# Six units' transposed keys: TensorE transposes and a copy in place of VectorE transposes and a trip through DRAM

## The chip, the cores and the metric

The kernel runs on one core of one Trainium2 chip. The metric is the device time of one execution in microseconds; before the change it is 614.58 us, the median of three runs (614.53 to 615.55). Engines are called by the names of the profile: PE is TensorE (PEld its weight loads), DVE is VectorE, ACT is ScalarE, POOL is GpSimd, SP the engine whose queue issues most of the DMAs.

## What is computed

A gated linear attention with a running state, and a SwiGLU block on its output, all in fp32. In the reference, cut to what matters:

```python
batch, n_heads, seq, head_dim = (4, 8, 768, 48)      # q, k, v, f_logit
n_tokens, d_model, d_ff = (3072, 384, 1536)
...
f = 1.0 / (1.0 + np.exp(-f_logit))
for t in range(S):
    state = f[:, :, t, :, None] * state + np.einsum('bhd,bhe->bhde', k[:, :, t], v[:, :, t])
    y[:, :, t] = np.einsum('bhd,bhde->bhe', q[:, :, t], state)
...
x = np.ascontiguousarray(attn_out.transpose(0, 2, 1, 3)).reshape(B * S, H * D)
g = x @ w_gate
silu = g * (1.0 / (1.0 + np.exp(-g)))
return (silu * (x @ w_val) @ w_out)
```

## The kernel before

**Units and chunks.** The sequence is cut into six chunks of 128 tokens (NCH = 6). A unit is one batch in one chunk, with all eight heads; units are numbered u = 4c + b, 24 in all. `attention(u)` computes one unit and is a Python generator: each `yield` ends a step, and the caller decides when the next step's instructions are put into the program. Eight heads are held as four pairs (HP = 4), two heads on 128 partitions.

**The steps of a unit** (from the third chunk on, c >= 2): the sigmoid of f (L555, ACT), a 32x32 block transpose of f on DVE (L561), the same of k (L568), the backward running product `tail` of the gates and its reciprocal (L572 to L577), the multiplication kT = k * tail (L582), the forward running product in the place of the gates (L596), the transpose of q (L599) and the multiplication into qT (L602). Then PE makes the scores of the pairs, sc = kT^T qT (L615, eight matmuls of 48 rows), DVE applies the causal mask (L628), PE adds the output y from the decayed state and the masked scores (L649, L653, or L674 for the last batch of a chunk), ACT copies y out (L657, L689), and PE adds the state's sum dS from `kt` and v (L694). `kt` is kT turned: tokens on the partitions, heads times 64 along the row. The last chunk needs no dS and no `kt`.

**Two ways to `kt`.** For most units PE transposes kT in four matmuls against the identity into a PSUM bank right after the scores (L616 to L619), and ACT copies the bank to SBUF (L626). Units 14 to 19 (`turned`, L584) do otherwise: DVE turns 32x32 blocks of kT into the room that qT will take (L589), four DMAs on SP's queue store that to DRAM (`turn`, L592), and after the scores one DMA reads it back in the other order as `kt` (L624). qT's own transpose (L599) has to wait until the four stores have read its room.

**The MLP of chunk c runs while the attention of chunk c+1 goes on.** The first chunk's MLP is plain. From the second on it uses sums of blocks: four triples of 15 products (`triple`, L954, names A, B, o, c for the banks that the products go to), each product two matmuls of 256 columns, then seven down products in fourteen halves (L1053, L1116). ACT copies the banks out as `c..` or `aside` tiles (L959; three `aside` rooms), DVE adds and subtracts them (L855, L858), ACT applies SiLU (L970) and DVE multiplies (L906).

**PSUM.** From the second chunk's MLP on there are two banks of kind A, one of kind B, two of kind o, and three in a pool of their own for y, dS and kt (`later`). Scores stand in banks borrowed from the kinds A and o (`score_bank`), as the table `SCORES` says.

**What sets the order.** A planner by due times: the pieces of the MLP carry an estimated duration (PRODUCT 0.86 us, DOWN 3.9 us), and each step of `attention` has a due time relative to the start of the MLP chunk beside which it runs. `chain(k, q, qmul, turn, head)` (L819) gives the times of a unit's DVE steps: k + STEPS, then `turn` (L589 and L592) and `head` (L596), both k + 3.5 where not given, then q (L599) and qmul (L602). `CHAINS` holds them by chunk and batch, `times` (L835) makes the list of a unit's steps. Whenever the planner's clock has passed a step's due time, `come_in` puts the step in. At the end `in_order` (L1283) pins each engine's instructions to the order in which they were put in, SP's queue among them. Otherwise the framework's scheduler may order what has no dependency.

The names that the change touches are `turn_pool` (L321), the steps L584 to L594 and L616 to L626, the state's sum's operand (L695), the numbers of steps in `attention_steps` (L715) and `run` (L1172), `STEPS`, `chain` and `CHAINS`, and the last call of `in_order`.

Of the kernel before, what the change touches and what calls it, by code (L numbers as in the profile page):

```python
# [9 lines left out]
FP32 = mybir.dt.float32  # L10
# [279 lines left out]
def short_path(ctx, tc, ident, least, judge, q, k, v, f_logit, moe_w_gate, moe_w_val, moe_w_out, out):  # L290
# [9 lines left out]
    nc = tc.nc  # L300
    B, H, S, D = q.shape
    C = 128
    NCH = S // C
    HP = H // 2
    W = 64
# [9 lines left out]
    SQUARES = 2  # L315
# [2 lines left out]
    const = ctx.enter_context(tc.tile_pool(name="const", bufs=1))  # L318
    att = ctx.enter_context(tc.tile_pool(name="att", bufs=1))
    ffn = ctx.enter_context(tc.tile_pool(name="ffn", bufs=2))  # L320
    turn_pool = ctx.enter_context(tc.tile_pool(name="turn", bufs=2, space=bass.MemoryType.DRAM))  # L321
    sums_pool = ctx.enter_context(tc.tile_pool(name="sums", bufs=1))

    early = ctx.enter_context(ExitStack())
# [25 lines left out]
    start = const.tile([128, HP * N1], FP32, tag="start", name="start")  # L350
# [42 lines left out]
    Q = 32  # L393
    NI = C // Q
# [9 lines left out]
    def v_of(u):  # L404
        return vs[u % (NV if units[u][1] < SQUARES else NV // 2)]
# [105 lines left out]
    def rows_of(par):  # L511
        return slice(W * par, W * par + D)
# [3 lines left out]
    def bank(name):  # L516
        return banks[-1].tile([128, 512], FP32, tag="a", name=name)
# [10 lines left out]
    def attention(u):  # L528
        b, c = units[u]
        fr, kr, qr = (raw[nm][u % NRAW] for nm in "fkq")  # L530
        v_ = v_of(u)
# [15 lines left out]
        def transposed(name, src):  # L547
            p = bank(name)
            for a in range(HP):
                nc.tensor.transpose(p[:, a * C:(a + 1) * C],  # L550
                                    src[:, 2 * a:2 * a + 2, :].rearrange("t r d -> t (r d)"), ident)
            return p.rearrange("p (a t) -> p a t", t=C)
# [3 lines left out]
        else:  # L556
            p = transposed("fTp", fr)
# [6 lines left out]
        kT = att.tile([128, HP, C], FP32, tag="kT", name="kT")  # L564
        qT = att.tile([128, HP, C], FP32, tag="qT", name="qT", bufs=2)
# [15 lines left out]
            qp = transposed("qTp", qr)  # L581
        nc.vector.tensor_tensor(kT, kp, pairs(tail, 2)[:, :, 0:C], ALU.mult)  # L582
        yield
        turned = (SQUARES + 1) * B + 1 < u < (NCH - 1) * B  # L584
        if turned:


            beside = qT.rearrange("p a t -> p (a t)").rearrange("p (i m) -> p i m", i=NI)
            nc.vector.transpose(beside.rearrange("p i (a e) -> p a i e", e=Q), kT.rearrange("p a (i e) -> p a i e", e=Q))  # L589
            turn = turn_pool.tile([Q, NI, HP, NI, Q], FP32, tag="turn", name="turn")  # L590
            for r in range(NI):
                nc.sync.dma_start(out=turn[:, :, :, r, :].rearrange("t i a e -> t (i a) e"),  # L592
                                  in_=beside[Q * r:Q * (r + 1)].rearrange("t i (a e) -> t (i a) e", e=Q))
        yield  # L594

        nc.vector.tensor_tensor_scan(gate[:, 0:n], gate[:, 0:n], start, 1.0, op0=ALU.mult, op1=ALU.add)  # L596
        yield
# [14 lines left out]
        for a in range(HP):  # L612
            for par in range(2):
                r = rows_of(par)
                nc.tensor.matmul(sc[par][:, a * C:(a + 1) * C], lhsT=kT[r, a, :], rhs=qT[r, a, :], start=True, stop=True)  # L615
        if c < NCH - 1 and not turned:  # L616
            p = bank("kt")
            for a in range(HP):
                nc.tensor.transpose(p[:, a * C:(a + 1) * C], kT[:, a, :], ident)  # L619
        yield  # L620
        if c < NCH - 1:
            kt = att.tile([128, HP * C], FP32, tag="kt", name="kt")
            if turned:
                nc.sync.dma_start(out=kt, in_=turn.rearrange("t i a r e -> i t (a r e)"))  # L624
            else:
                nc.scalar.copy(kt, p)  # L626
        for par in range(2):
            nc.vector.tensor_tensor(A[:, par], sc[par].rearrange("p (a t) -> p a t", t=C),  # L628
                                    causal.unsqueeze(1).broadcast_to((128, HP, C)), ALU.mult)
# [7 lines left out]
        if c and b < B - 1:  # L637
# [8 lines left out]
            for a in range(HP):  # L646
                for par in range(2):
                    r = rows_of(par)
                    nc.tensor.matmul(place(a, par), lhsT=decayed[r, a, :], rhs=qT[r, a, :],  # L649
                                     start=a < 2, stop=False, skip_group_check=True)  # L650
            for par in range(2):
                for a in range(HP):
                    nc.tensor.matmul(place(a, par), lhsT=v_[:, 2 * a + par, :], rhs=A[:, par, a, :],  # L653
                                     start=False, stop=a >= HP - 2, skip_group_check=True)
# [3 lines left out]
            for h in range(H):  # L658
                a, par = h // 2, h % 2
                f = h * D  # L660
                while f < (h + 1) * D:
                    n = min((h + 1) * D, (f // 128 + 1) * 128) - f
                    r = W * (a % 2) + f - h * D
                    nc.sync.dma_start(out=xT[c][f % 128:f % 128 + n, f // 128, b * C:(b + 1) * C],
                                      in_=yT[r:r + n, par, a // 2 * C:(a // 2 + 1) * C])
                    f += n
        else:
# [15 lines left out]
            for par in range(2):  # L683
                for n in range(DM // Q):
                    h = n // per * 2 + par
# [5 lines left out]
        if c < NCH - 1:  # L691
            p = bank("dS")
            for h in range(H):
                nc.tensor.matmul(p[W * (h % 2):W * (h % 2) + W, (h // 2) * D:(h // 2 + 1) * D],  # L694
                                 lhsT=kt[:, h * W:(h + 1) * W], rhs=v_[:, h, 0:D], start=True, stop=True)  # L695
            dS = p[:, 0:HP * D].rearrange("p (a d) -> p a d", d=D)
        if c >= SQUARES and u + 2 < len(units):
            load(u + 2, "v")
# [13 lines left out]
    def attention_steps(c):  # L712

        runs = [attention(c * B + b) for b in range(B)]
        parts = [3, 6, 3, 3]  # L715
        order = sorted((2 * b + s, b, n) for b in range(B) for s, n in enumerate(parts))
        return [lambda b=b, n=n: [next(runs[b]) for _ in range(n)] for _, b, n in order]

# [2 lines left out]
    def in_order(since, engines):  # L721

        start = len(traced)
        while traced[start - 1] is not since:
            start -= 1
        for engine in engines:
            keep_order([ins for ins in traced[start:] if ins.engine == engine])

    def keep_order(mine):
        for a, b in zip(mine, mine[1:]):  # L730
            tc.add_manual_dep(b, a.name, mybir.DependencyInfo(mybir.DependencyClass.NoSync,
                                                              mybir.DependencyReason.DATA), reason="order")
# [80 lines left out]

    STEPS = (-1.3, 0, 1.3, 2.8)
    TRIPLE = PRODUCT * 15

    def chain(k, q, qmul, turn=None, head=None):  # L819
        return (*[k + t for t in STEPS], turn or k + 3.5, head or k + 3.5, q, qmul)  # L820

    whole = NJ * TRIPLE + 7 * DOWN
    between = [n * TRIPLE - 0.05 for n in range(NJ)]
# [4 lines left out]
        *[((down[10] - whole, "A"), (between[1], "o"), (between[3], "o"), (down[3], "A"))] * (NCH - 4)))}  # L828
    CHAINS = {c: chains for c, chains in zip(range(2, NCH), (
        (chain(2.6, 4, 9), chain(14.5, 20, 23), chain(30, 37, 44), chain(57.4, 59, 61)),  # L830
        (chain(-12, -8.5, -5), chain(3.5, 6, 9), chain(16, 28, 33, 21.5, 23.5), chain(40.1, 53, 55, 44.5, 52)),
        *[(chain(-19.4, -11.2, -9.5), (-7.5, -6.3, 1.3, 2.2, 3.2, 5.5, 8, 10), chain(16, 28, 33, 21.5, 23.5), chain(40.1, 53, 55, 44.5, 52))] * (NCH - 4)))}
    LAST = 72.5

    def times(c):  # L835
# [327 lines left out]
    mark = traced[-1]  # L1163
    keep_warm(5)
    first = [attention(b) for b in range(B)]
    done = [0] * B

    def run(b, *steps):
        for s in steps:
            assert done[b] == s  # L1170
            done[b] += 1
            for _ in range((3, 1, 5, 3, 3)[s]):  # L1172
                next(first[b])

    def load_ahead(u):
# [5 lines left out]
        if u + NRAW == B:  # L1181
            load(u + NRAW, "fkq")

    run(0, 0, 1, 2)
    load_ahead(0)
    for b in range(1, B):
        if b == 1:
            run(1, 0)
            keep_warm(6)
        run(b, 1)  # L1190
        run(b - 1, 3)
        run(b, 2)
        load_ahead(b)
        if b + 1 < B:
            run(b + 1, 0)
        else:
            sizes.pop(0)()
        run(b - 1, 4)
# [6 lines left out]

    hidden, last = mlp_plain(0)
    steps = attention_steps(1)
    sigmoid_ahead(B)
    joins.pop(0)()
# [38 lines left out]
    mark = traced[-1]  # L1248
    waiting = []
    for c in range(2, NCH):  # L1250
        for b in range(B):
            run = attention(c * B + b)
            waiting += [((c - 2) * whole + t, lambda run=run: next(run)) for t in times(c)[b]]
# [26 lines left out]
            now += took  # L1280
    for g in lagging:
        g()
    in_order(mark, (mybir.EngineType.PE, mybir.EngineType.DVE, mybir.EngineType.Activation, mybir.EngineType.Pool, mybir.EngineType.SP))  # L1283


@with_exitstack
def kernel(
# [22 lines left out]
    def judge(bank):  # L1310
# [12 lines left out]
        yield  # L1323

    short_path(tc, ident, least, judge, *args)
    with tc.If(redo[0] > 0):
        general_path(tc, *args)
# [32 lines left out]
```

## Time and profile before

| | us |
|---|---|
| median of three runs | 614.58 |
| the profiled execution | 615.55 |
| its span on the core | 613.7 |
| L619, PE transposes of kT: 56, each record | 0.273 |
| L626, ACT copy of kt, 14 | 0.586 |
| L589, DVE transpose of kT, 6 | 0.704 |
| L596, DVE running product, 24, mean | 1.224 |
| L592, stores of `turn`, issue of each of 24 | 0.626 |
| L592, issue to landing, median | 2.6 |
| L624, load of `kt`, issue of each of 6 | 0.602 |

The profile is one execution, and its span lies within that execution's time. A row "x56" is the number of instructions, and for one instruction the record's duration is given. Records of matmuls overlap, so the distance from one group's start to the next one's is what a group takes on PE. In the timeline a line has start, duration, engine, source line, operation and tile; lines of one kind that follow each other are merged. An fp32 matmul shows as two records there (the eight score matmuls of a unit as "x16", a product's two as "x4"), a transpose as one ("x4" for a unit's four).

### The profile page before, as it was taken

To read this page: it belongs to the slowest core of one execution; us is meant where nothing else is said; L and a number is where in the kernel's file an instruction comes from. 1 tells how busy PE (TensorE), PEld (TensorE's weight loads), DVE (VectorE), ACT (ScalarE), POOL (GpSimd) and SP (SyncE) were. 2 spreads that over 40 slices of the span, in tenths; PEclk is the share of its full clock that TensorE was granted. 3 is DMA by queue.
4 is the path that set the end of the run, shared out by engine and by line. 5 is a ranking of instruction groups with operands and counts; after the bars stand their busy time and mean duration, and the time that the engine had idled before them with its cause. 6 is when DMAs were issued, how large, how long until landed. Compare 5 with 4: busy or idle time off the path is not lost.

```text
span 613.7 us, 10812 instructions
## 1 busy us (share of the span) xinstructions
PE 596.7 (97%) x4036; PEld 488.6 (80%) x4036; DVE 499.5 (81%) x882; ACT 285.1 (46%) x526; POOL 7.6 (1%) x51
## 2 busy tenths in 40 slices
PE   7799999999999999999999999999999999999996
PEld 4654545666888799888899988899988899988895
DVE  7799989878999996989997889996879991566731
ACT  2375646312776520576731376641276730366600
POOL 1000000000000000000000000000000000000000
PEclk9899999999999999999999999999999999999999
DMA  9999582005322144324235344145313100100001
GB/s 150 246 209 284 175 249 79 1 14 154 85 54 69 27 97 115 113 53 96 52 96 129 98 111 108 33 112 118 110 43 91 27 5 10 52 2 2 1 0 58
DMA packets 109143, 54.10 MB, mean 88 GB/s; under 512 B 68761, under 2 KB 102169, under 8 KB 109081
## 3 DMA queue, kind: packets, MB, share of 16 engines
q1 hardware_dynamic: 107064, 50.56, 34.6%
q10 hardware_dynamic: 2016, 2.75, 1.2%
q8 instruction: 34, 0.56, 0.4%
q14 instruction: 29, 0.23, 0.1%
HBM read 44.04 MB, written 6.29 MB: 82 GB/s over the span
## 4 chain that ended last, share of the span: by engine, by line
PE 85%; DVE 7%; DMA 3%; ACT 2%; issue 1%; SPq 1%; ACTq 0%; DVEq 0%
PE o L1053 19%; PE A L954 14%; PE B L954 11%; PE gate L752 5%; PE val L752 5%; PE o L775 5%; PE o L954 5%; PE c L954 4%; PE sc L615 4%; PE o L1116 3%; PE y L653 2%; PE y L674 2%; PE dS L694 1%; PE y L649 1%; DVE c L858 1%; DMA fraw<-in_f_logit_dram 1%
## 5 line engine op out<-in xcount | busy, mean ns | idle before, releaser
L954 PE MATMUL A<-xs,w_both 128*128 128x256 f32 x240 | 62.5, 383 | 1.2 <-ACT aside L959 1.2
L1053 PE MATMUL o<-w_out,h 128*128 128x192 f32 x360 | 62.0, 327 | 0.5 <-DVE h L906 0.5
L1053 PEld LDWEIGHTS o<-w_out,h 128*128 128x128 f32 x360 | 58.7, 190 | 1.7 <-DVE h L906 0.8
L959 ACT COPY c<-A 128x512 f32<-128x512 f32 x40 | 23.3, 583 | 66.8 <-PE A L954 66.8
L954 PEld LDWEIGHTS A<-xs,w_both 128*128 128x128 f32 x240 | 44.5, 190 | 9.1 <-ACT aside L959 2.8
L855 DVE TENSOR_TENSOR c<-c,aside 128x512 f32<-128x512 f32 x60 | 41.4, 691 | 9.8 <-ACT aside L959 8.4
L959 ACT COPY aside<-A 128x512 f32<-128x512 f32 x60 | 35.0, 583 | 28.9 <-PE A L954 28.9
L906 DVE TENSOR_TENSOR h<-h,c 128x256 f32<-128x256 f32 x100 | 41.1, 419 | 7.9 <-ACT h L970 7.7
L970 ACT ACTIVATE h<-c 128x256 f32<-128x256 f32 x100 | 39.2, 416 | 9.0 <-DVE c L855 5.8
L858 DVE TENSOR_TENSOR c<-c,aside 128x512 f32<-128x512 f32 x60 | 41.3, 688 | 2.0 <-ACT aside L959 1.7
L954 PE MATMUL B<-xs,w_both 128*128 128x256 f32 x160 | 41.2, 380 | 0.7 <-ACT aside L959 0.7
L1053 PE MATMUL o<-ws,h 128*128 128x192 f32 x240 | 41.5, 328 | 0.2 <-DVE A L628 0.2
L954 PE MATMUL c<-xT,w_both 128*128 128x256 f32 x160 | 41.2, 380 | 0.5 <-DVE c L858 0.5
L954 PE MATMUL A<-xs,extra 128*128 128x256 f32 x160 | 41.2, 380 | 0.0
L954 PE MATMUL B<-xT,extra 128*128 128x256 f32 x160 | 41.1, 379 | 0.0
L628 DVE TENSOR_TENSOR A<-sc,causal 128x512 f32<-128x512 f32 x48 | 30.8, 684 | 11.3 <-PE sc L615 11.3
L959 ACT COPY aside<-B 128x512 f32<-128x512 f32 x60 | 35.0, 584 | 10.2 <-PE B L954 7.2
L1053 PEld LDWEIGHTS o<-ws,h 128*128 128x128 f32 x240 | 39.1, 190 | 0.8 <-DVE A L628 0.4
L858 DVE TENSOR_TENSOR c<-o,c 128x512 f32<-128x512 f32 x40 | 27.7, 693 | 10.2 <-ACT h L970 5.8
L954 PEld LDWEIGHTS B<-xs,w_both 128*128 128x128 f32 x160 | 30.2, 190 | 5.2 <-ACT aside L959 1.1
L954 PEld LDWEIGHTS c<-xT,w_both 128*128 128x128 f32 x160 | 30.2, 190 | 5.1 <-DVE c L858 0.9
L954 PEld LDWEIGHTS A<-xs,extra 128*128 128x128 f32 x160 | 30.3, 190 | 4.4 <-ACT c L959 0.3
(137 smaller groups left out, 1139.8 us busy)
## 6 DMA issues: line engine op xcount, KB each, us to landing
fsquares<-in_f_logit_dram SPq DMA_DIRECT2D x64, 96.0 KB, 2.6
ksquares<-in_k_dram SPq DMA_DIRECT2D x64, 96.0 KB, 2.4
qsquares<-in_q_dram SPq DMA_DIRECT2D x64, 96.0 KB, 2.3
v<-in_v_dram SPq DMA_DIRECT2D x24, 192.0 KB, 3.5
w<-in_moe_w_gate_dram SPq DMA_DIRECT2D x6, 768.0 KB, 6.1
w<-in_moe_w_val_dram SPq DMA_DIRECT2D x6, 768.0 KB, 5.7
w<-in_moe_w_out_dram SPq DMA_DIRECT2D x6, 768.0 KB, 5.6
out_dram<-ob ACTq DMA_DIRECT2D x14, 192.0 KB, 2.1
```

The source lines that it names most:

```text
L615: nc.tensor.matmul(sc[par][:, a * C:(a + 1) * C], lhsT=kT[r, a, :], rhs=qT[r, a, :], start=True, stop=True)
L628: nc.vector.tensor_tensor(A[:, par], sc[par].rearrange("p (a t) -> p a t", t=C), causal.unsqueeze(1).broadcast_to((128, HP, C)), ALU.mult)
L752: nc.tensor.matmul(p, lhsT=w[:, j, i, :], rhs=xT[c][:, i, :], start=(i == 0), stop=(i == KT - 1))
L775: nc.tensor.matmul(p, lhsT=hidden_tile(h, n // 2)[:, n % 2 * 2 + b // 2, b % 2 * C:(b % 2 + 1) * C], rhs=w_out[:, j, :], start=(n == 0), s ...
L855: nc.vector.tensor_tensor(dst, a, b, ALU.add)
L858: nc.vector.tensor_tensor(dst, a, b, ALU.subtract)
L906: lagging.append(lambda: f(*args))
L954: nc.tensor.matmul(p[name][:, n, :], lhsT=weights_of[a][:, n, j, :], rhs=tokens[b], start=fresh and n == 0, stop=True, skip_group_check=True)
L959: nc.scalar.copy(t, p[name])
L970: nc.scalar.activation(dst, src[:, 0, :], AF.Silu)
L1053: nc.tensor.matmul(p[:, n, :], lhsT=lhsTs[j][:, n * C:(n + 1) * C], rhs=rhs[:, j, :], start=first and j == order[0] and n == 0, stop=j == ...
L1116: nc.tensor.matmul(p, lhsT=hidden_tile(h, j)[:, 2, n * C:(n + 1) * C], rhs=b22[:, j, :], start=j == order[0], stop=j == order[-1])
```

## The change

Units 14 to 19 lose their own way to `kt` and take that of the others: four PE transposes after the scores, and the copy on ACT. The step between L582 and L596 is gone, so a unit has one step less, and the numbers of steps follow. The due time of the running product (L596) is now k + 3.5 for every unit, where units had a `head` of their own (batches 2 and 3 of the fourth chunk on); in the fifth and sixth chunks the due times of batch 0 and batch 1 are set anew. SP's queue is left out of the last `in_order`. `kt` has the same elements in the same places, declared as heads by 64.

```diff
-    turn_pool = ctx.enter_context(tc.tile_pool(name="turn", bufs=2, space=bass.MemoryType.DRAM))
...
         nc.vector.tensor_tensor(kT, kp, pairs(tail, 2)[:, :, 0:C], ALU.mult)
         yield
-        turned = (SQUARES + 1) * B + 1 < u < (NCH - 1) * B
-        if turned:
-            beside = qT.rearrange("p a t -> p (a t)").rearrange("p (i m) -> p i m", i=NI)
-            nc.vector.transpose(beside.rearrange("p i (a e) -> p a i e", e=Q), kT.rearrange("p a (i e) -> p a i e", e=Q))
-            turn = turn_pool.tile([Q, NI, HP, NI, Q], FP32, tag="turn", name="turn")
-            for r in range(NI):
-                nc.sync.dma_start(out=turn[:, :, :, r, :].rearrange("t i a e -> t (i a) e"),
-                                  in_=beside[Q * r:Q * (r + 1)].rearrange("t i (a e) -> t (i a) e", e=Q))
-        yield
         nc.vector.tensor_tensor_scan(gate[:, 0:n], gate[:, 0:n], start, 1.0, op0=ALU.mult, op1=ALU.add)
...
-        if c < NCH - 1 and not turned:
+        if c < NCH - 1:
             p = bank("kt")
             for a in range(HP):
                 nc.tensor.transpose(p[:, a * C:(a + 1) * C], kT[:, a, :], ident)
         yield
         if c < NCH - 1:
-            kt = att.tile([128, HP * C], FP32, tag="kt", name="kt")
-            if turned:
-                nc.sync.dma_start(out=kt, in_=turn.rearrange("t i a r e -> i t (a r e)"))
-            else:
-                nc.scalar.copy(kt, p)
+            kt = att.tile([128, H, W], FP32, tag="kt", name="kt")
+            nc.scalar.copy(kt, p.rearrange("t (h d) -> t h d", d=W))
...
-                                 lhsT=kt[:, h * W:(h + 1) * W], rhs=v_[:, h, 0:D], start=True, stop=True)
+                                 lhsT=kt[:, h, :], rhs=v_[:, h, 0:D], start=True, stop=True)
...
-        parts = [3, 6, 3, 3]
+        parts = [3, 5, 3, 3]
...
-    STEPS = (-1.3, 0, 1.3, 2.8)
+    STEPS = (-1.3, 0, 1.3, 2.8, 3.5)
-    def chain(k, q, qmul, turn=None, head=None):
-        return (*[k + t for t in STEPS], turn or k + 3.5, head or k + 3.5, q, qmul)
+    def chain(k, q, qmul):
+        return (*[k + t for t in STEPS], q, qmul)
...
-        (chain(-12, -8.5, -5), chain(3.5, 6, 9), chain(16, 28, 33, 21.5, 23.5), chain(40.1, 53, 55, 44.5, 52)),
-        *[(chain(-19.4, -11.2, -9.5), (-7.5, -6.3, 1.3, 2.2, 3.2, 5.5, 8, 10), chain(16, 28, 33, 21.5, 23.5), chain(40.1, 53, 55, 44.5, 52))] * (NCH - 4)))}
+        (chain(-12, -8.5, -5), chain(3.5, 6, 9), chain(16, 28, 33), chain(40.1, 53, 55)),
+        *[(chain(-19, -14.5, -11), (-7.5, -6.3, 1.5, 2.5, 3.3, 5, 8), chain(16, 28, 33), chain(40.1, 53, 55))] * (NCH - 4)))}
...
-            for _ in range((3, 1, 5, 3, 3)[s]):
+            for _ in range((3, 1, 4, 3, 3)[s]):
...
-    in_order(mark, (mybir.EngineType.PE, mybir.EngineType.DVE, mybir.EngineType.Activation, mybir.EngineType.Pool, mybir.EngineType.SP))
+    in_order(mark, (mybir.EngineType.PE, mybir.EngineType.DVE, mybir.EngineType.Activation, mybir.EngineType.Pool))
```

## The prediction

> **What bounds the kernel now.** The page comes first: its span, its engines and the chain that ended last.
>
> ```profile
> span 613.7 us, 10812 instructions
> PE 596.7 (97%) x4036; PEld 488.6 (80%) x4036; DVE 499.5 (81%) x882; ACT 285.1 (46%) x526; POOL 7.6 (1%) x51
> PE 85%; DVE 7%; DMA 3%; ACT 2%; issue 1%; SPq 1%; ACTq 0%; DVEq 0%
> ```
>
> TensorE is busy for 97% of the span and makes 85% of the chain. That is a mean over the program, so the second view is the stretch that the change touches. The chunks of the MLP that begin at 250.0 and 343.3 us hold all six units concerned; the columns are PE, PEld, DVE, ACT and POOL busy, then the granted clock, the DMA share and GB/s. Beside them stand all waits of TensorE in this stretch (sum, times, longest).
>
> ```profile
> 250.00:343.30 93.30, 93.01 (x689) 83.16 (x689) 82.45 (x143) 46.80 (x90) 0.84 (x5) 1.00 0.36 92
> 343.30:437.20 93.90, 93.61 (x690) 83.73 (x689) 81.46 (x146) 46.71 (x89) 0.84 (x5) 1.00 0.37 91
> ...
> PE A L954 <- ACT aside L959: 0.6, 2, 0.3
> ```
>
> Of 187.2 us TensorE is idle for 0.6, at the full clock. So whatever TensorE gets to do here is paid in full, and what VectorE or the DMA queue is relieved of is worth at most that 0.6.
>
> The Trainium skill (Perfetto Trace Analysis, Identifying the Most-Contended Engine) speaks against this reading: matmul busy time is a bad measure, and the busy share of weight loads is to be used. That share is 83.16 of 93.30 us here, and by it some 10 us per chunk would be free and would swallow what is added. I follow the rows: in the records below each group begins where the one before lets it.
>
> **What the change takes away.** Six units (14 to 19) have turned kT by a VectorE transpose (L589), four stores to DRAM (L592) and one load back (L624), all on SP's queue. The rows:
>
> ```profile
> L589 DVE STREAM_TRANSPOSE qT<-kT x6: 700/704/711, 277.7 to 397.3; 128x512 f32<-128x512 f32 x6
> DVE qT L599 <- DMA turn<-qT: 5.5, 3, 3.3
> L624 SPq DMA_DIRECT2D kt<-turn x6: 591/602/672, 301.5 to 417.4; - x6
> ```
>
> VectorE is relieved of 6 x 0.704 = 4.2 us and of three waits of 5.5 us together, SP of 30 issues of some 0.6 us. No wait of TensorE on L624's kt is in the list above: the trip through DRAM is hidden. Worth on the path: 0, at most the 0.6 us.
>
> **What it adds on TensorE.** Four transposes for each of the six units, 24, right after that unit's scores. Unit 13 has them now, at the place in its triple of products where unit 14 has none. The two stretches (start, duration):
>
> ```profile
> 262.71 0.67 PE L649 MATMUL y<-qT,decayed 48*64 48x128 f32 x16
> ...
> 264.78 1.16 PE L615 MATMUL sc<-qT,kT 48*128 48x128 f32 x16
> 265.87 0.66 PE L619 MATMUL kt<-idf,kT 128*128 128x128 f32 x4
> 266.37 1.03 PE L954 MATMUL A<-xs,w_both 128*128 128x256 f32 x4
> 267.23 1.03 PE L954 MATMUL B<-xs,w_both 128*128 128x256 f32 x4
> ...
> 292.64 0.67 PE L649 MATMUL y<-qT,decayed 48*64 48x128 f32 x16
> ...
> 294.71 1.16 PE L615 MATMUL sc<-qT,kT 48*128 48x128 f32 x16
> 295.80 1.13 PE L954 MATMUL A<-xs,w_both 128*128 128x256 f32 x4
> 296.77 1.03 PE L954 MATMUL B<-xs,w_both 128*128 128x256 f32 x4
> ```
>
> The transposes hold the next group back by 266.37 - 265.87 = 0.50 us. But without them the first group after the scores takes 0.97 instead of 0.86 us (295.80 to 296.77 against 266.37 to 267.23), because its weights are not loaded ahead. So from y to the product B it is 267.23 - 262.71 = 4.52 us with and 296.77 - 292.64 = 4.13 us without: 0.39 net. In the down products (units 15, 16, 19) the same comparison is unit 10 against unit 15: from the scores to the 25th record of the down products 220.77 - 215.28 = 5.49 us with; without, 12 records end at 320.15 and 12 more take 1.95, so 322.10 - 317.01 = 5.09: 0.40 net. I take 0.40. The bounds for a unit are 0.39 and the whole record of 0.66; six units make 2.4 us (2.3 to 4.0).
>
> The Trainium skill (VectorE: DVE Perf Modes, The three transpose paths) gives 390 ns for one such transpose on TensorE, in bf16. By that price 24 would be an estimated 9.4 us. The row of four that follow each other in 0.50 us, 0.125 each in fp32, decides.
>
> **What it adds on ScalarE.** Six copies of 128x512 from PSUM (L626, 586 ns), 3.5 us. ScalarE is busy half of the time here, but the copy stands between copies that empty banks which TensorE waits for. The cover is shown by unit 13: there c<-A starts at 267.43, kt at 267.92 and c<-B at 268.39, done at 268.99, while B is next written 2.6 us after 267.23, at about 269.8. TensorE lists no wait there. Slack some 0.8 us; if it were gone, one unit would pay up to 0.59, six 3.5. I take 0, with 3.5 as the other end. The bank that kt takes from the pool of three is the one of the same unit round's first y; it is read by ScalarE's L657 copy from 294.18 and 316.24 us on, and the transposes would start at 295.8 and 318.1, at least 1 us after its first half is read. The products dS that read kt come a whole unit later (16 us or more).
>
> **What it moves.** On VectorE the scan L596 now follows the multiplication L582 at once, which puts 1.23 us ahead of work that stood before it: for units 14, 15, 18 and 19 net 1.23 - 0.70 = 0.5 us, for units 22 and 23, which had no L589, the full 1.2. Late next are the subtractions that free "aside" tiles, the SiLU that waits for them, and then the copy that frees bank B. At unit 23 the copy of aside<-B starts at 492.41 and would end about 0.8 us later, at 493.8, against the product in B at 493.94: just in time. At the end of a third triple the last hidden tile is ready at 310.4, and TensorE asks for it after 16 records of 0.1625 us (24 in 3.90) from 308.99, at 311.6: 1.2 us of cover for 0.4 to 0.6 of delay. Cost 0; if the cover fails, some 0.3 us in each of three chunks. In the first chunk of this phase L596 passes one subtraction; the tile it frees is asked for at 160.31, two microseconds later: 0. The wait of 0.3 before the A product at 354.04 follows ScalarE's table load at 351.80, which stays.
>
> **SP's queue** is no longer held to the program's order. In the built program the first of four loads of f for units 17 and 21 passes the xT copies of units 14 and 18, and the flag's load passes the last two stores of the output. The f load waits for L561 of unit 16, done at 318.7, while the xT copies behind it could start at 316.6: they end some 2.5 us late, at about 326, read by the next chunk's token sums at 341. Then come v and the other f loads at about 327 to 329, where they now go out at 327.84 to 331.66 and ScalarE waits for them until 333.65: no later than now. For unit 21 the same makes them some 1.5 us later than now (ScalarE waits until 425.58); late next is only the copy of y at 427.62, whose bank nothing asks for in the 20 us after: 0. Some k loads pass two output stores: earlier, 0. The flag's load at the end lies beside the last stores, which are issued by 608.4 and take 4.1 us to land: 0; if it came after them, the row of an issue, 0.6.
>
> **Sum.** Profiled execution: 615.55 (span 613.7 and 1.85 around it) + 2.4 = 617.95. That execution is the slowest of three; the median is 0.97 lower, so 614.58 + 2.4 = **617.0 us**.
>
> **Rivals.** (1) New waits on ScalarE's copy: the extra 0.59 shows at all six units, bank B and A come late: 614.58 + 2.4 + 3.5 = 620.5. For it: ScalarE empties B only just in time where VectorE is full (277.43 against the product at 277.59). Against: unit 13, and units 10 and 12. Chance 0.11. (2) The change does not cost what it seems: the 24 transposes slip into the weight-load gaps at the changeovers: 614.6. For it only the 0.10 per changeover, already counted; against it, both pairs. Chance 0.09. (3) Faster: VectorE is the hidden pacer through the two chunks, and its 4.2 + 5.5 = 9.7 us come off: 614.58 + 2.4 - 9.7 = 607.3. It decides from 2.4 us of shortened TensorE waits on; the place would be 324 to 334 us, where VectorE waits 3.26 us for the store. Against: TensorE is idle 0.6 us in both chunks, and at that place not at all. Chance 0.03.
>
> **How the numbers follow.** The forecast has 0.77. Its own spread: 614.58 + 2.3 - 0.6 = 616.3 to 614.58 + 4.0 = 618.6, with some 0.3 for the spread of the runs. 615.9 to 618.8 holds most of it and a part of (1). A measurement of this kernel can tell about 0.2%, 1.2 us, from no change: slower is the forecast and (1), 0.88; within is (2), 0.09; faster is (3), 0.03.
>
> **What would show it.** L619 with 80 instead of 56 transposes at 0.125 us spacing; the chunks at 250 and 343.3 us longer by about 1.2 us each (units 14, 15 and 16 have their scores in the first, 17, 18 and 19 in the second); TensorE's waits there still under 1 us; L626 x20; no wait of VectorE on L599. I am wrong if TensorE waits on aside or c copies after the new L626s, or if the chunks do not grow.

## The result, and the profile after

The changed kernel takes 617.50 us (median of four runs, 616.78 to 617.63), the kernel before, measured with it, 614.83 us in four runs (614.53 to 615.55): ratio 1.0039, 95% interval 1.0022 to 1.0057. It is slower by some 2.7 us, against a forecast of 2.4 (617.0, range 615.9 to 618.8).

First the page of the profile after, in the lines that answer those of before: span, engines, chain by engine.

```profile
span 615.9 us, 10835 instructions
PE 600.4 (97%) x4060; PEld 491.1 (80%) x4060; DVE 495.7 (80%) x876; ACT 288.5 (47%) x532; POOL 7.6 (1%) x51
PE 80%; DVE 10%; ACT 4%; DMA 2%; issue 2%; SPq 2%; POOL 0%; ACTq 0%; DVEq 0%; POOLq 0%
```

TensorE has 24 instructions more and is busy 3.7 us longer, VectorE has 3.8 us less to do and the span is 2.2 us longer. Next the two chunks that the change touches (columns as before: length, PE, PEld, DVE, ACT, POOL busy, clock, DMA share, GB/s).

```profile
249.03:343.52 94.49, 94.20 (x702) 84.38 (x701) 80.59 (x140) 48.49 (x93) 0.84 (x5) 1.00 0.32 82
343.52:439.30 95.78, 95.06 (x702) 84.84 (x701) 79.93 (x143) 48.12 (x92) 0.84 (x5) 1.00 0.28 73
```

And all waits of TensorE in them (sum, times, longest):

```profile
PE A L939 <- ACT aside L944: 0.6, 2, 0.3
PE o L1038 <- ACT ob L1064: 0.4, 1, 0.4
```

The lines have new numbers: L939 was L954 (products), L944 the copies L959, L1038 the down products L1053, L1064 the copy of ob L1079, L607 and L611 are the transposes and copy of kt (L619, L626), L649 the xT copies (L664). The first chunk grew from 93.30 to 94.49, by 1.19 us: three units' transposes. The second grew from 93.90 to 95.78, by 1.88, of which 0.43 is idle time: a wait on `ob` that the kernel before does not have.

Unit 14 in the timeline after (start, duration, engine, line) shows what the transposes take:

```profile
293.75 1.16 PE L603 MATMUL sc<-qT,kT 48*128 48x128 f32 x16
294.84 0.66 PE L607 MATMUL kt<-idf,kT 128*128 128x128 f32 x4
295.33 1.03 PE L939 MATMUL A<-xs,w_both 128*128 128x256 f32 x4
296.19 1.03 PE L939 MATMUL B<-xs,w_both 128*128 128x256 f32 x4
```

The view of the tile kt says how often they and the copies now come (min, median and longest duration in ns, then the first and last start):

```profile
L607 PE MATMUL kt<-idf,kT x80: 272/273/331, 12.5 to 413.3; 128*128 128x128 f32 x80
L611 ACT COPY kt<-kt x20: 559/588/595, 13.2 to 413.7; 128x512 f32<-128x512 f32 x20
```

From the scores to the product B it is 296.19 - 293.75 = 2.44 us, against 296.77 - 294.71 = 2.06 before: 0.38. A single record lasts 0.273 us, but four of them hold the next group back by 0.49, and some 0.10 of that comes back, since the first product then takes 0.86 instead of 0.97.

**How the runs are read from here on.** A whole run's time varies by more than 1 us, much of it from the start-up: in the profiles, the scores of the first four units already stand up to 2.3 us apart from those of before. In the profile of before the granted clock is 0.50 from 20.4 to 23.7 us, in that of after it is 1.00 there. So beside each run's time I give how much longer than before the stretch from unit 13's first score matmul (264.78 us before) to unit 21's (452.43) is. It holds all six units and nothing of the start, and the granted clock is 1.00 throughout it in all profiles but those of e7 and e8. For the changed kernel, the shift of each unit's scores against before:

| unit | 13 | 14 | 15 | 16 | 17 | 18 | 19 | 20 | 21 |
|---|---|---|---|---|---|---|---|---|---|
| after | -0.96 | -0.96 | -0.57 | -0.18 | 0.22 | 0.61 | 1.01 | 2.10 | 2.10 |

Five steps of 0.39 to 0.40 us, one for each unit's transposes, and one of 1.09 behind unit 19: 0.39 for its transposes and 0.70 that the prediction does not have. In all +3.06.

### The profile page after: what moved, and what is told of

It is laid out like the page before. It is cut to its first block, busy times and chain, and to the rows that moved or that the text cites. A ratio compares the mean times of both kernels' runs of the same rounds, so it can differ in the third digit from the quotient of the medians.

```text
span 615.9 us, 10835 instructions
## 1 busy us (share of the span) xinstructions
PE 600.4 (97%) x4060; PEld 491.1 (80%) x4060; DVE 495.7 (80%) x876; ACT 288.5 (47%) x532; POOL 7.6 (1%) x51
## 4 chain that ended last, share of the span: by engine, by line
PE 80%; DVE 10%; ACT 4%; DMA 2%; issue 2%; SPq 2%; POOL 0%; ACTq 0%; DVEq 0%; POOLq 0%
PE o L1038 17%; PE A L939 15%; PE B L939 12%; PE o L939 5%; PE o L760 5%; PE c L939 4%; PE val L737 4%; PE sc L603 3%; PE gate L737 3%; PE o L1101 3%; PE y L638 2%; PE y L659 1%; SPq L649 1%; PE y L634 1%; PE kt L607 1%
## 5 line engine op out<-in xcount | busy, mean ns | idle before, releaser
L939 PE MATMUL A<-xs,w_both 128*128 128x256 f32 x240 | 62.2, 382 | 1.2 <-ACT aside L944 1.2
L1038 PE MATMUL o<-w_out,h 128*128 128x192 f32 x360 | 61.9, 327 | 0.5 <-DVE h L891 0.5
L1038 PEld LDWEIGHTS o<-w_out,h 128*128 128x128 f32 x360 | 58.7, 190 | 1.6 <-DVE h L891 0.8
L944 ACT COPY c<-A 128x512 f32<-128x512 f32 x40 | 23.3, 583 | 65.5 <-PE A L939 65.5
L939 PEld LDWEIGHTS A<-xs,w_both 128*128 128x128 f32 x240 | 44.6, 190 | 8.7 <-ACT aside L944 2.8
L840 DVE TENSOR_TENSOR c<-c,aside 128x512 f32<-128x512 f32 x60 | 41.3, 689 | 11.2 <-ACT aside L944 10.1
L944 ACT COPY aside<-A 128x512 f32<-128x512 f32 x60 | 35.0, 583 | 27.4 <-PE A L939 27.4
L939 PE MATMUL B<-xs,w_both 128*128 128x256 f32 x160 | 41.2, 380 | 0.7 <-ACT aside L944 0.7
L939 PE MATMUL c<-xT,w_both 128*128 128x256 f32 x160 | 41.2, 380 | 0.5 <-DVE c L843 0.5
L1038 PE MATMUL o<-ws,h 128*128 128x192 f32 x240 | 41.3, 327 | 0.2 <-DVE A L613 0.2
L939 PE MATMUL A<-xs,extra 128*128 128x256 f32 x160 | 41.2, 380 | 0.0
L939 PE MATMUL B<-xT,extra 128*128 128x256 f32 x160 | 41.1, 380 | 0.0
L944 ACT COPY aside<-B 128x512 f32<-128x512 f32 x60 | 35.0, 584 | 11.0 <-PE B L939 6.5
L1038 PEld LDWEIGHTS o<-ws,h 128*128 128x128 f32 x240 | 39.1, 190 | 0.6 <-DVE A L613 0.4
L840 DVE TENSOR_TENSOR c<-c,o 128x384 f32<-128x384 f32 x15 | 8.3, 554 | 34.6 <-PE o L1038 34.6
L939 PEld LDWEIGHTS B<-xs,w_both 128*128 128x128 f32 x160 | 30.3, 190 | 5.1 <-ACT aside L944 1.1
L939 PEld LDWEIGHTS c<-xT,w_both 128*128 128x128 f32 x160 | 30.3, 190 | 5.1 <-DVE c L843 0.9
```

The source lines that it names most:

```text
L840: nc.vector.tensor_tensor(dst, a, b, ALU.add)
L939: nc.tensor.matmul(p[name][:, n, :], lhsT=weights_of[a][:, n, j, :], rhs=tokens[b], start=fresh and n == 0, stop=True, skip_group_check=True)
L944: nc.scalar.copy(t, p[name])
L1038: nc.tensor.matmul(p[:, n, :], lhsT=lhsTs[j][:, n * C:(n + 1) * C], rhs=rhs[:, j, :], start=first and j == order[0] and n == 0, stop=j == ...
```

## The experiments

Each is an edit of the kernel before or after; times are medians, with the ratio to before and its 95% interval. "Stretch" is the growth from unit 13 to unit 21 just described.

| run | time, us | ratio | stretch, us |
|---|---|---|---|
| after | 617.50 | 1.0022 to 1.0057 | +3.06 |
| e12, after again | 618.47 | 1.0033 to 1.0070 | +3.52 |
| e1, SP's order kept | 617.21 | 1.0021 to 1.0046 | +2.64 |
| e2, before with SP free | 614.66 | 0.9984 to 1.0003 | 0.00 |
| e3, old due times | 617.46 | 1.0022 to 1.0046 | +2.62 |
| e4, kt alone | 617.18 | 1.0020 to 1.0047 | +2.62 |
| e9, copy on VectorE | 617.30 | 1.0024 to 1.0051 | +2.36 |
| e5, copy twice | 618.20 | 1.0029 to 1.0064 | +3.66 |
| e6, transposes twice | 619.90 | 1.0056 to 1.0092 | +5.25 |
| e10, DRAM from unit 13 | 615.24 | 0.9992 to 1.0016 | -0.11 |
| e11, DRAM from unit 12 | 615.50 | 1.0001 to 1.0025 | +0.71 from unit 12 |
| e7, DRAM from unit 12, old times | 620.12 | 1.0049 to 1.0088 | +5.5 from unit 12 |
| e8, DRAM from unit 8 | 632.74 | 1.0266 to 1.0307 | not read |

**The change in its parts: e1 to e4.** e1 is the changed kernel with SP's queue pinned, e2 the kernel before with it free:

```diff
# e1 (on after); e2 is the reverse, on before
-    in_order(mark, (mybir.EngineType.PE, mybir.EngineType.DVE, mybir.EngineType.Activation, mybir.EngineType.Pool))
+    in_order(mark, (mybir.EngineType.PE, mybir.EngineType.DVE, mybir.EngineType.Activation, mybir.EngineType.Pool, mybir.EngineType.SP))
```

> The changed kernel with one thing undone: SP's queue is again held to the program's order in the last in_order. My theory: the six units' transposes cost 2.4 us, and 0.7 us more come from one load of f that passed unit 18's xT copies (VectorE's room for yT stays taken, GpSimd's memset, ScalarE's two diagonal copies and its copy of ob come late, and TensorE waits 0.43 us for that copy at 423.8). Then this one takes 2.4 us more than the kernel before, about 0.7 less than the changed kernel, and no wait of TensorE on L1064's copy is listed. Rival A, that ScalarE's added copies of kt made that wait: no change against the changed kernel, 3.1 more than before, the wait still there. Rival B, that the scans put earlier on VectorE made it: the same as A.

> The kernel before with one thing changed: SP's queue is left out of the last in_order. Here no load of f passes an xT copy; some stand ahead of the turn stores, some stores of the output later, and the flag's load behind the last stores. My theory: nothing on the path, within 0.3 us of the kernel before. Rival: the flag's load behind the last stores lengthens the tail by its own time, some 0.6 us.

e3 is the changed kernel with the due times of before, e4 the kernel before with nothing changed but the way to kt:

```diff
# e3 (on after)
-    def chain(k, q, qmul):
-        return (*[k + t for t in STEPS], q, qmul)
+    def chain(k, q, qmul, head=None):
+        return (*[k + t for t in STEPS[:4]], head or k + 3.5, q, qmul)
...
-        (chain(-12, -8.5, -5), chain(3.5, 6, 9), chain(16, 28, 33), chain(40.1, 53, 55)),
-        *[(chain(-19, -14.5, -11), (-7.5, -6.3, 1.5, 2.5, 3.3, 5, 8), chain(16, 28, 33), chain(40.1, 53, 55))] * (NCH - 4)))}
+        (chain(-12, -8.5, -5), chain(3.5, 6, 9), chain(16, 28, 33, 23.5), chain(40.1, 53, 55, 52)),
+        *[(chain(-19.4, -11.2, -9.5), (-7.5, -6.3, 1.3, 2.2, 5.5, 8, 10), chain(16, 28, 33, 23.5), chain(40.1, 53, 55, 52))] * (NCH - 4)))}
# e4 (on before)
-        turned = (SQUARES + 1) * B + 1 < u < (NCH - 1) * B
+        turned = False
```

> The changed kernel with the due times of the kernel before (running product at k + 7.5 and k + 11.9 for batches 2 and 3, batches 0 and 1 of the last two chunks as before); SP's queue free. In this order the load of f does not pass the xT copies. My theory: 2.4 us more than before, 0.7 less than the changed kernel, no wait on L1064's copy. Rival B (scans earlier on VectorE cost by themselves): the same, so this run and e1 only tell them apart together: if both lose the wait, it is the queue; if only this one does, it is VectorE. Rival A (ScalarE's copies): 3.1 more than before.

> The kernel before with one thing changed: no unit is turned through DRAM, all take TensorE's transposes and ScalarE's copy; old due times, SP's queue in order. My theory: the six units cost 0.40 us each on TensorE and nothing else, 2.4 us more than before. Rival 1 of the prediction (ScalarE's copies exposed): up to 5.9 more. Rival 2 (the transposes slip into weight-load gaps): the same as before.

e4, the way to kt alone, comes to +2.62 and 617.18 us: 2.36 in six steps and 0.26 at one other place (last section). The due times (e3 against e1) are worth nothing to within 0.02 us of the stretch; e3 leaves SP's queue free as well, but in its order no load of f passes unit 18's xT copies (they go out from 411.71, the loads of f from 418.67). A free SP queue does nothing to the kernel before (e2, 0.00), but the changed kernel has 0.42 more with it than without (3.06 against 2.64). Without the 0.28 us that e1 loses at another place and after does not (last section), it is 0.70. The whole times of e1, e3, e4 and after cannot be told apart; it is the stretch that separates them.

**Where the 0.70 us arise: after, e12 and e1.** The place is 412 to 424 us, and the timeline shows it. After (issues of SP's queue, POOL's memset, ScalarE, TensorE; in brackets the idle time before and its releaser):

```profile
412.57 0.31 SPq L426 DMA_DIRECT2D fsquares<-in_f_logit_dram  x1
412.98 6.22 SPq L649 DMA_DIRECT2D xT<-yT  x10
...
422.08 0.42 POOL L542 MEMSET diagonal<- 128x384 f32 x1 [12.07 <-DMA xT<-yT]
422.53 0.71 ACT L544 COPY diagonal<-decayed 48x192 f32<-48x192 f32 x2 [8.29 <-POOL diagonal L542]
423.27 0.48 ACT L1064 COPY ob<-o 128x384 f32<-128x384 f32 x1
...
423.80 4.17 PE L1038 MATMUL o<-ws,hs 128*128 128x192 f32 x24 [0.43 <-ACT ob L1064]
```

and e1, with SP's queue in the program's order:

```profile
411.95 6.21 SPq L649 DMA_DIRECT2D xT<-yT  x10
...
418.89 1.95 SPq L426 DMA_DIRECT2D fsquares<-in_f_logit_dram  x4
...
419.70 0.42 POOL L542 MEMSET diagonal<- 128x384 f32 x1 [9.23 <-DMA xT<-yT]
420.15 0.71 ACT L544 COPY diagonal<-decayed 48x192 f32<-48x192 f32 x2 [5.45 <-POOL diagonal L542]
420.89 0.48 ACT L1064 COPY ob<-o 128x384 f32<-128x384 f32 x1
...
423.66 4.06 PE L1038 MATMUL o<-ws,hs 128*128 128x192 f32 x24
```

The first load of f for unit 21 has to wait for unit 20's transpose of f, and stands ahead of unit 18's ten xT copies, which issue 1.03 us later by the clock than in e1. What is late next is not their data, but their source: yT lies in the room (the tag "x", one buffer) that the `diagonal` of unit 19 wants. The memset waits for the xT copies, ScalarE's copies into the diagonal wait for the memset, and behind them in ScalarE's order stands the copy that empties the bank o that TensorE needs. In e1 `ob` is copied by 421.37, 2.3 us before TensorE starts at 423.66; after, it ends at 423.75 and TensorE is held. The wait of 0.43 delays the group by 0.60 against before (the last section comes back to this); the remaining 0.1 of the 0.70 is lost in the records behind it.

e12 runs the changed kernel once more.

> The changed kernel once more, unaltered, to tell its own SP order's share from noise. Theory (the first load of f for unit 21 stands ahead of unit 18's copies to xT, and the room that they hold is wanted for the diagonal): TensorE's wait of 0.4 us on ob at 423.8 recurs, and units 13 to 21 are again 3.0 to 3.1 us longer, against 2.6 with the queue in order. Rival (chance in one execution): no wait on ob, 2.4 to 2.6 longer.

The wait of TensorE on `ob` recurs, longer:

```profile
413.47 6.21 SPq L649 DMA_DIRECT2D xT<-yT  x10
...
423.04 0.42 POOL L542 MEMSET diagonal<- 128x384 f32 x1 [12.55 <-DMA fsquares<-in_f_logit_dram]
...
424.76 3.52 PE L1038 MATMUL o<-ws,hs 128*128 128x192 f32 x20 [0.90 <-ACT ob L1064]
```

The stretch is +3.52, and unit 20 comes 1.57 us later than unit 19 where 0.40 is the transposes' share: 1.17 us for this wait. (The bracket at the memset names a load of f; what lands just ahead of it is the last xT copy, issued at 419.09 and landed 3.7 us later.) In its six runs e12 takes 618.47 us, 3.9 more than the kernel before beside it (614.58).

So the wait recurs in both profiled executions of this order, and in none of those in which the load of f stays behind the copies (e1, e3, e4, e5, e6, e9). But the order is only a part of it. The memset follows the end of the issues (419.20 after, 419.68 in e12) by 2.9 and 3.4 us, against 1.5 in e1 (418.16 to 419.70): from issue to landing the slowest of the ten copies takes 3.7 us in after and in e12, and 1.8 in e1. With e1's 1.8 us for the last copy, `ob` would be copied some 1 us before TensorE asks for it (an estimate from these rows: about 422.3 against 423.4 after, 422.8 against 423.9 in e12), so the later issue alone would not have held TensorE. A slow landing is not peculiar to this order: in e6, with SP's queue in order, the slowest of unit 18's copies takes 3.7 us too, and TensorE does not wait. Both together make the 0.70 and the 1.17. Whether this order also brings the slow landing to the last copies is open. A room of its own for the diagonal was not run.

**What the transposes cost: e6.** On e1, with the transposes of units 14 to 19 made twice into the same bank:

```diff
-            for a in range(HP):
+            for a in [*range(HP)] * (2 if u > 13 else 1):
                 nc.tensor.transpose(p[:, a * C:(a + 1) * C], kT[:, a, :], ident)
```

> The changed kernel with SP's queue in order (as e1), and TensorE makes each of the 24 transposes of units 14 to 19 twice into the same bank: 24 transposes more. My theory: each takes 0.125 us of TensorE and all are on the path, 24 x 0.125 = 3.0 us above e1, 5.6 above the kernel before from unit 13's scores to unit 21's. By the record's duration (0.273 us each) it would be 6.6 above e1; rival 2 (gaps between weight loads take them) 0 above e1.

```profile
295.21 1.09 PE L607 MATMUL kt<-idf,kT 128*128 128x128 f32 x8
296.14 1.03 PE L939 MATMUL A<-xs,w_both 128*128 128x256 f32 x4
```

Eight of them take 296.14 - 295.21 = 0.93 us. The stretch is 5.25 - 2.64 = 2.61 longer than e1's: 0.435 for four more, 0.109 each, a little under the 0.125 (3.0 in all) that was expected. TensorE has no new wait; all of what it is given here is paid.

**What the copy costs: e5 and e9.** e5, on e1, makes ScalarE's copy of kt twice for units 14 to 19. e9, on e1, has VectorE make it once in ScalarE's place, behind the masks:

```diff
# e5
             nc.scalar.copy(kt, p.rearrange("t (h d) -> t h d", d=W))
+            if u > 13:
+                nc.scalar.copy(kt, p.rearrange("t (h d) -> t h d", d=W))
# e9
-            nc.scalar.copy(kt, p.rearrange("t (h d) -> t h d", d=W))
+            if u < 14:
+                nc.scalar.copy(kt, p.rearrange("t (h d) -> t h d", d=W))
         for par in range(2):
             nc.vector.tensor_tensor(A[:, par], sc[par].rearrange("p (a t) -> p a t", t=C),
                                     causal.unsqueeze(1).broadcast_to((128, HP, C)), ALU.mult)
+        if 13 < u and c < NCH - 1:
+            nc.vector.tensor_copy(kt, p.rearrange("t (h d) -> t h d", d=W))
```

> The changed kernel with SP's queue in order (as e1), and ScalarE copies kt twice for units 14 to 19: 3.5 us more on ScalarE, nothing else. My theory (ScalarE has room, TensorE alone pays): from unit 13's scores to unit 21's this takes as much longer than the kernel before as e1 does, 2.6 us, within 0.6. Rival (the copies' cover is thin): each second copy is paid, up to 3.5 us more, 6.1 together.

e5's second copy is free at units 15, 16 and 19, in the down products, and costs 0.42 to 0.48 us at units 14, 17 and 18, which stand in the triples. The waits of TensorE from 255 to 440 us in e5:

```profile
PE A L941 <- ACT aside L946: 0.6, 2, 0.3
PE A L941 <- ACT c L946: 0.5, 3, 0.2
```

and in its timeline the place at unit 14, where ScalarE's copy follows the table load for SiLU:

```profile
300.60 0.56 ACT L946 COPY c<-A 128x512 f32<-128x512 f32 x1
301.22 1.13 PE L941 MATMUL A<-xs,extra 128*128 128x256 f32 x4 [0.15 <-ACT c L946]
```

The three waits come to 0.5 us, but the three units lose 1.3 (the last section comes back to this). After, with one copy, the same c<-A copy ends at 300.17 (299.60 and 0.57), and the product starts on time at 300.51. So ScalarE has at most 0.34 us to spare there, and a second copy of kt, which in e5 starts 0.62 after the first (297.27 and 297.89), does not fit.

> The changed kernel with SP's queue in the program's order, and for units 14 to 19 the copy of kt on VectorE, right behind the unit's masks, instead of ScalarE. That gives VectorE back some 0.6 us for each of the six units. Theory (TensorE alone pays, VectorE has the cover): units 13 to 21 longer by 2.4 to 2.6 us than before, 617.0 to 617.2, as with the copy on ScalarE. Rival (VectorE is the hidden pacer, or its room was used up by the scans that come earlier): TensorE waits on c or aside from VectorE, and the stretch is up to 3.5 us longer than that, some 620. Rival of the ScalarE copy: if it is the copy on ScalarE that costs the 0.2 to 0.3 us above six times 0.39, the stretch is 2.36 longer.

e9 gives VectorE back the 0.7 us per unit that the change took from it; its timeline at unit 14:

```profile
297.33 0.68 DVE L617 COPY kt<-kt 128x512 f32<-128x512 f32 x1
```

The list of TensorE's waits from 255 to 440 us is this one line:

```profile
PE A L942 <- ACT aside L947: 0.6, 2, 0.3
```

It waits for nothing new, and the stretch grows by 2.36: six steps of 0.38 to 0.40 and nothing else. VectorE's time is not what sets the pace here.

**More units through DRAM: e7, e8, e10, e11.** If each unit with transposes pays 0.39 us, then sending further units through DRAM should win as much. e7 and e8 widen `turned` in the kernel before, without touching due times:

```diff
# e7; e8 has SQUARES * B - 1 < u
-        turned = (SQUARES + 1) * B + 1 < u < (NCH - 1) * B
+        turned = (SQUARES + 1) * B - 1 < u < (NCH - 1) * B
```

> The kernel before with units 12 and 13 turned through DRAM as well (eight units in place of six). My theory: 2 x 0.40 = 0.8 us less than the kernel before, if the trip is as well hidden there. Rival: VectorE's transposes and the wait of L599 for the stores come into a fuller VectorE (82% busy in that chunk) and give it back: 0, or more by up to 2 x 0.7.

> The kernel before with units 8 to 13 turned as well (all twelve that have a state's sum to make from the third chunk on). My theory's linear part: 6 x 0.40 = 2.4 us less. But units 8 to 11 stand beside the MLP chunk in which TensorE waits for VectorE and ScalarE (1.2 to 1.5 us of waits now) and the weight sums are made; 4 x 0.70 us of VectorE more there may be paid in full. Expected between 2.4 us less and 1 us more than before; I take 1 us less.

Both are slower. VectorE's transpose of q (L599) has to wait until the stores have read its room; in e7, unit 12's: 

```profile
259.41 0.71 DVE L589 STREAM_TRANSPOSE qT<-kT 128x512 f32<-128x512 f32 x1
...
264.41 1.12 DVE L599 STREAM_TRANSPOSE qT<-qsquares 128x512 f32<-128x512 f32 x1 [3.18 <-DMA turn<-qT]
```

VectorE stands 3.18 us and all behind it comes late, until TensorE, at unit 13's scores, waits 1.70 us for qT and 0.98 for c, which it does not before. Behind these waits the profile has a granted clock of 0.50 for some 6 us (the third column from the end), and a product takes about twice its time there; the kernel before has 1.00 at this place.

```profile
268.00:274.00 6.00, 5.44 (x22) 4.59 (x23) 4.54 (x8) 2.31 (x5) 0.00 (x0) 0.50 0.41 112
270.56 2.07 PE L954 MATMUL A<-xs,w_both 128*128 128x256 f32 x4
272.43 1.91 PE L954 MATMUL B<-xs,w_both 128*128 128x256 f32 x4
```

From A to B it is 1.87 us, where the kernel before takes 0.86 (266.37 to 267.23). So of e7's 5.5 us some 2.7 are waits and some 3 are the lower clock (an estimate: half of 6); the gain of 0.8 that was expected stands against them. e7's six runs spread from 617.85 to 621.71. e8 has more of both: 9.3 us of waits on qT in the whole program, against 1.5 before, 3.7 us on the load of kt itself, and a granted clock of 0.50 in three stretches of at least 6.7, 10.1 and 3.3 us (from 164.7, 236.4 and 284.2 on). e10 turns unit 13 alone with a chain that leaves 3 us for the stores; e11 turns 12 too, with its chain earlier:

```diff
# e10; e11 also has (-13.9, -13.5, -12.2, -11.2, -10.8, -8.5, -6, -3.5) for chain(-12, -8.5, -5), and turned from unit 12 on
-        turned = (SQUARES + 1) * B + 1 < u < (NCH - 1) * B
+        turned = (SQUARES + 1) * B < u < (NCH - 1) * B
...
-        (chain(-12, -8.5, -5), chain(3.5, 6, 9), chain(16, 28, 33, 21.5, 23.5), chain(40.1, 53, 55, 44.5, 52)),
+        (chain(-12, -8.5, -5), (0.9, 1.0, 1.3, 2.2, 3.2, 5.5, 8, 10), chain(16, 28, 33, 21.5, 23.5), chain(40.1, 53, 55, 44.5, 52)),
```

In both, unit 13's backward product is formed before unit 12's state is decayed, in the same room, so that unit 12's state is decayed by unit 13's gates; the instructions are the same in number and size.

> The kernel before, with unit 13 going through DRAM too, and due times for unit 13 that leave its four stores 3 us ahead of the transpose of q (as batch 1 of the later chunks has them). Theory (0.39 us of TensorE for each unit that has the transposes): unit 13 to unit 21 0.4 us shorter than before, 614.2 in all, not to be told from no change by the times, but by the starts of the scores. Rival (VectorE has no room for it at unit 13: it waits for the stores, and TensorE waits for a tile from it): 0 to 1 us longer.

> As the run from unit 13 on, and unit 12 through DRAM too, with its chain of VectorE steps some 2 us earlier and 4.8 us between the turning of k and the transpose of q (in the earlier run that took units 12 and 13 with unchanged due times VectorE waited up to 4.6 us for the stores and the stretch lost 5 us). Theory (only VectorE's wait for the stores was to blame there): no wait of TensorE on qT, 0.8 us shorter than before by unit 21, 613.8. Rival (the trip takes longer at unit 12, or VectorE is full there): TensorE waits for qT or c again, 1 to 5 us longer.

e10's stretch is 0.11 us shorter: TensorE's 0.39 is gained, and 0.28 are lost in unit 13's scores, in which no wait is recorded. e11's stretch, from unit 12 on, is 0.71 us longer instead of 0.8 shorter. Half of the 1.5 us between them is lost from unit 12's scores to unit 13's, with a wait that its list of TensorE's waits from 255 to 440 us has new:

```profile
PE B L954 <- ACT aside L959: 0.6, 1, 0.6
```

The other half has no recorded wait: 0.44 in unit 13's scores and 0.28 in a product B before unit 21 (the last section comes back to this). So the earlier chain removes most of e7's loss, the low clock with it (it is 1.00 from 247 to 270 us), but not all: from 235 to 340 us VectorE still stands 8.6 us for the stores, in four units. Neither beats the kernel before, and no version that was run does.

## Why the prediction was right, and where it was not

- **What bounds it: right.** TensorE's idle time in the two chunks was 0.6 us and is 1.0, and the 24 transposes lengthened the span. e6 gives it 24 more, and every one is paid. The contrary rule that the prediction weighed (the Trainium skill, Perfetto Trace Analysis, Identifying the Most-Contended Engine: judge TensorE's headroom by MFU, the share of its peak work rate, and by the busy share of weight loads) does not fit here as the prediction used it: the weight loads alone left some 10 us per chunk, and by that neither step would show.
- **What it takes away, worth 0: right.** The 4.2 us of VectorE and its waits of 5.5 did come off (in the two chunks VectorE is busy 160.5 us instead of 163.9, and no wait on L587, the old L599, is left), and nothing is gained. e9 puts six copies of 0.68 us back on VectorE and loses nothing.
- **Transposes at 0.40 a unit, 2.4 in all: right.** Six steps of 0.38 to 0.40, 2.36 in e9, where nothing else is added. The record's 0.66 as the upper bound was far too high: after the first four, one more transpose costs 0.109 (e6). The 390 ns apiece that the Trainium skill has for one in bf16 (VectorE: DVE Perf Modes, The three transpose paths) is not what a run of four or eight fp32 ones costs here.
- **ScalarE's copies at 0: right, but the cover was measured at the wrong bank.** "Slack some 0.8 us" was read at bank B; the tightest place is the A product behind the SiLU table load, with at most 0.34 (after, beside e5). One copy fits, a second does not.
- **Moves on VectorE, 0: right** (e3 with the old due times against e1 with the new). The just-in-time places did not slip: there is no new wait on aside tiles.
- **SP's queue, 0: the one term that was wrong.** The prediction followed the f load that passes the xT copies of unit 14 and unit 18, asked who reads xT ("read by the next chunk's token sums at 341") and when f arrives, and for unit 21 said "late next is only the copy of y at 427.62". It did not ask who waits for the room that the copies free. At unit 18 that is the diagonal, and through ScalarE's order the bank o: 0.70 us in the profiled execution, 1.17 in the second, both times with the last copies landing late as well. At unit 14 nothing waited, as predicted, and the flag's load at the end cost nothing that can be seen (the span after unit 23's scores is 110.3 us before and 110.4 after).
- **The sum.** 2.36 + 0.70 = 3.06 in the stretch. The forecast for the profiled execution was 617.95, and it took 617.63, because its start was 0.96 us shorter than in the profile of before: two errors that nearly cancel there. Against the median, 2.4 was forecast and 2.7 measured, with an interval of 1.4 to 3.5.
- **The rivals.** (1), all six copies exposed, would have given 3.5 more in the stretch: none is, and it takes a second copy to expose three. (2), transposes in the gaps, is refuted by the steps of 0.39. (3), VectorE as the pacer, is refuted by the result itself, in which VectorE is rid of these 9.7 us and the kernel is slower, and by e9.

The queue's 0.70 us is in no term of the forecast. That the time lies well within the range all the same is in part luck: the room came from the transposes' upper bound of 4.0, which was itself too high.

What stays open: in e1, e3 and e4 the stretch is 0.26 to 0.28 longer than six times 0.39, all at one point, and e6 loses 0.28 there too (last section), and why the last xT copies landed late in after and e12.

## What to carry to other kernels

Where one engine is idle for less than a microsecond in a hundred, price what is added to it by the distance to the next group with and without it, not by the record's duration, and expect to pay it in full; what was taken from the others here was worth nothing. When a transfer is moved in a queue, ask two questions of each one it is put ahead of: who reads what that brings, and who is waiting for the room it reads from. Measure an engine's slack at the tightest of the places that a repeated instruction goes to, not at the first one.

## What was not expected of the hardware

- In these runs a wait of TensorE cost more than its recorded idle time. 0.43 us of waiting delayed the group by 0.60 and the stretch by 0.70, 0.90 by 1.07 and 1.17; the three waits of 0.5 in e5 cost 1.3. After the wait on ob in after, the group's weight loads start with its first matmul (both at 423.80), where in e1 they start 0.16 us ahead of it (423.50 and 423.66).
- In e7 and e8 TensorE's granted clock fell to 0.50 for 3 to 10 us at a time in the middle of the program, in e7 just behind 2.7 us of waits. So e7 lost about as much again as its waits. Which wait is long enough for it was not measured; after the 0.90 us in e12 the clock stayed at 1.00.
- TensorE sometimes loses 0.28 us at once with no wait in the records. In e1, e3, e4 and e6 it is in the product B after 355 us (356.89 in e6), at a granted clock of 1.00; here in e1's timeline:

```profile
355.40 1.03 PE L939 MATMUL B<-xT,extra 128*128 128x256 f32 x4
356.57 1.13 PE L939 MATMUL A<-xT,w_both 128*128 128x256 f32 x4
```

From B to the next A it is 1.17 us; before it is 0.90 (355.00 to 355.90), after 0.89. In e7 and e11 the same 0.28 is lost from unit 20's scores to unit 21's, in e10 in unit 13's scores (1.43 where they take 1.16). e9, whose TensorE program is the same as e1's, does not have it. No run settles what it is.
